# Softcapped attention with routed experts on one core: the score tile split into four one-bank tiles for the tail, and TensorE's share of the softmax sums cut to two head groups

## The chip, the cores and the metric

The kernel runs on one core of a Trainium2 chip. The metric is device time in microseconds, the median of several executions. The profile is of one further execution, taken by the hardware profiler.

## The reference, cut to what matters

Eight batches, twelve heads, 448 positions, head width 64. The attention output of a batch is a matrix of 448 rows and 768 columns. The router takes the 128 rows with the highest score, sends them through a two-layer network (768 to 1024 to 768), and adds the gated result to those rows.

```
scores = cap * tanh((q @ k.T) / sqrt(64) / cap)            # cap = 30
attn   = exp(scores - max); attn = attn / (sum(attn) + 1e-9)
x[b]   = attn @ v                                          # heads side by side: 448 x 768
s      = x[b] @ w_gate
top    = the 128 rows of largest s
out[b] = x[b];  out[b, top] += sigmoid(s[top]) * (relu(x[b, top] @ w1) @ w2)
```

With a cap of 30 the exponential needs no maximum taken off (the kernel tests the cap at run time and takes its fast branch); the sums are divided out at the end.

## The kernel before, in words

**Head groups and steps.** Four heads of one batch form a "double"; there are 24 doubles, three to a batch. A double has seven steps, each a block of 64 key positions for its four heads. Scores are kept transposed: key positions on the partitions, 448 queries along the row.

**The attention pipeline.** Two steps make a pair, 84 pairs in all. For a pair TensorE writes eight score matmuls (`scores_mm`, L372) into the tile `psS`, which is four PSUM banks in one tile; ScalarE takes tanh of all four banks in one instruction into a slot `p` (L842) and then the exponential in place (L850). There is one `psS`, so the scores of the next pair wait for the tanh of this one. Eight value matmuls a pair (`values_mm`, L381) accumulate into two banks, `psV`. The ring `p` has four slots.

**The sums.** The softmax sum over the key positions is taken in two ways (`sums_proc`). VectorE adds the steps of a double into a tile `e` (L400 the first addition, L410 the others), and TensorE sums `e` over the partitions with 16 small matmuls against a column of ones (L423). For some doubles the last two steps are left out of `e`, and TensorE sums them directly, 16 more matmuls of the same kind for each step. Before, that is done as long as the planner has no time yet for the last weight of `w2`.

**The rest of a double.** The sums are copied (`sm`), turned (L435) and inverted (`rec`, L443, L446); the value banks are copied to `xT` (L390), turned on TensorE (L469, banks `psT` and `psH`), scaled into `xn` by VectorE (L483), stored, and multiplied with the gate weights (L508). After three doubles of a batch the routing runs: totals (L530, L532), a turn (L542), a comparison of all rows with all (L557, L562), a one-hot matrix (L592), a picking matmul (L601), and an indirect DMA from GpSimd that gathers the rows (L625).

**The experts.** The gathered rows are turned (L641) and split into a high and a low part (L390, L653). The first layer is two groups of 18 matmuls (L698), the second two groups of 24 (L735), a VectorE instruction combines (L751), and an indirect DMA scatters (L777). The weights are split into high and low parts by VectorE as well (L325, L328), 14 pieces, in the first quarter of the run.

**What sets the order.** The program is written out beforehand by a planner inside the kernel (`Sim`, `Front`): every piece of work is a task with an engine, a planned duration and dependencies, and the planner emits instructions in the order in which its clocks reach them. Each engine then runs its list in that order; semaphores are set by the framework, per tile. `Front.policy` fills TensorE's time between attention steps with expert work and with the turns of finished doubles, at a rate that leaves a reserve for the time after attention. When the last value step is planned, `finish_attention` hands the banks of `psV` and the four banks of `psS` to the ring of free banks, so that the remaining expert work (the tail) has eight banks instead of two.

Of the kernel before, what the change touches and what calls it, by code (L numbers as in the profile page):

```python
# [8 lines left out]
F32 = mybir.dt.float32  # L9
# [7 lines left out]
P = 128  # L17
# [195 lines left out]
def allocate(tc, K):  # L213
    cp = K.const

    def t(name, shape, dt=F32):
        return cp.tile(shape, dt, name=name)

    S, CP, NCH = K.S, K.CP, K.NCH
    K.cap = t("capc", [P, 1])  # L220
    K.ident = t("ident", [P, P])
    K.fast = t("fast", [1, 1], I32)
    K.sq = t("sq", [1, 1])
    K.sc = t("sc", [P, 1])
    K.wts = {}
    for nm, n, m in (("w1", K.ND, K.F), ("w2", K.NF, K.DM)):
        for part in "hl":
            K.wts[nm + part] = t(nm + part, [P, n, m], F32R)
    K.wg = t("wg", [CP, K.DM])
    K.iota = t("iota", [CP, P])  # L230
    K.ids = t("ids", [CP, NCH])
    K.vals = [t(f"vals{i}", [CP, 4, NCH], F32R) for i in range(2)]
    K.before = t("before", [CP, S], BF16)
    K.ones = t("ones", [P, 63])
    K.part = [t(f"part{i}", [CP, K.NG, NCH]) for i in range(2)]
    K.jk, K.jt = t("jk", [CP, S], BF16), t("jt", [CP, S], BF16)
    K.work = K.stack.enter_context(tc.tile_pool(name="work", bufs=1))

    def ring(name, n, shape, dt=F32):
        return Ring([t(f"{name}{i}", shape, dt) for i in range(n)])  # L240

    K.q = ring("q", 3, [P, 2, S])
    K.k = ring("k", 3, [P, 2, S])
    K.v = ring("v", 2, [P, K.NS, 2, HD])
    K.p = ring("p", 4, [P, 2, 2, S])
    K.e = ring("e", 2, [P, 2, S])
    K.xT = ring("xT", 6, [P, S])
    K.sm = ring("sm", 2, [P, CP])
    K.xn = ring("xn", 2, [CP, NCH, 4 * K.D])
    K.rec = ring("rec", 2, [CP, NCH, 4])  # L250
    K.row = ring("row", 1, [CP, S])
    K.sel = ring("sel", 1, [CP, NCH, P], F32R)
    K.score = ring("score", 2, [CP, NCH])
    K.rk = ring("rk", 2, [CP, 3, NCH])
    K.xe = ring("xe", 2, [P, K.DM])
    K.idx = ring("idx", 3, [P, 1], I32)
    K.gt = ring("gt", 3, [P, 1])
    K.xs = Ring([(t("xh", [P, K.ND, P], F32R), t("xl", [P, K.ND, P], F32R))])
    K.hs = Ring([t("hs", [P, 1024])], free=False)
    K.hp = Ring([None], free=False)  # L260
    K.stages = [Ring([o]) for o in (K.hs.slots[0].obj, "mh", "ml")]

    def bank(tag, shape):
        pool = K.stack.enter_context(tc.tile_pool(name="ps" + tag, bufs=1, space=PSUM))
        return pool.tile(shape, F32, tag=tag, name="ps" + tag)

    K.S4 = bank("S", [P, 4, 512])
    K.acc = [Ring([bank(f"V{i}", [P, 512])]) for i in range(2)]
    K.banks = Ring([bank(c, [P, 512]) for c in "TH"])


def load_flag(tc, K, cap):
# [122 lines left out]
def sums_proc(tc, K, D):  # L395

    nc = tc.nc
    sim = K.sim
    yield [D.exp[0], D.exp[1]]
    e = yield Task("DVE", 1004, lambda t: nc.vector.tensor_tensor(  # L400
        t.slots[0].obj, D.P[0], D.P[1], op=ALU.add), deps=D.exp[:2], take=[K.e], refs=[1],
        reads=[D.pslot[0], D.pslot[1]], prio=1.5, kind="add")
    slot = e.slots[0]
    direct = []
    for s in range(2, K.NS):
        yield [D.exp[s]]
        if K.weights["w2"].t is None and s >= K.NS - 2:
            direct.append(s)
            continue
        e = yield Task("DVE", 1004, lambda t, s=s: nc.vector.tensor_tensor(  # L410
            slot.obj, slot.obj, D.P[s], op=ALU.add), deps=[e, D.exp[s]], reads=[D.pslot[s]],
            prio=1.5, kind="add")
    rec = K.recs[D.d]

    def sums(t):
        ps = t.slots[0].obj
        parts = [slot.obj] + [D.P[s] for s in direct]
        todo = [(part, n) for part in parts for n in range(K.NCH)]
        for i, (part, n) in enumerate(todo):
            for r in range(2):  # L420
                for j in range(2):
                    at = 32 * (2 * r + j)
                    nc.tensor.matmul(ps[at:at + 32, :K.CP], lhsT=K.ones[HALF[r], 31 - n:63 - n],  # L423
                                     rhs=part[HALF[r], j, n * K.CP:(n + 1) * K.CP],
                                     start=(i == 0), stop=(i == len(todo) - 1))

    s = yield Task("PE", 770 + 748 * len(direct), sums, deps=[e] + [D.exp[s] for s in direct],
                   take=[K.banks, K.sm], refs=[1, 1], shape=COLSUM,
                   reads=[slot] + [D.pslot[s] for s in direct], prio=(0, D.d), kind="sums")
    bank, sm = s.slots  # L430
    c = yield copy_task(tc, K.CP, lambda t: sm.obj, lambda t: bank.obj[:, :K.CP], deps=[s],
                        reads=[bank], prio=2, kind="smcopy")

    def turn(t):
        nc.tensor.transpose(t.slots[0].obj[:K.CP, :P], sm.obj, K.ident)  # L435

    t = yield Task("PE", 120, turn, deps=[c], take=[K.banks, K.rec], refs=[1, 2], reads=[sm],
                   prio=(0, D.d), kind="turnsums")
    tb, rec.slot = t.slots

    def scale(t):
        r = rec.slot.obj
        nc.vector.tensor_scalar(  # L443
            r, tb.obj[:K.CP, :P].rearrange("p (i r) -> p r i", i=4)[:, :K.NCH, :],
            1.0 + EPS, None, op0=ALU.mult)
        nc.vector.reciprocal(r, r)  # L446

    r = yield Task("DVE", 370, scale, deps=[t], reads=[tb], prio=1, kind="rec")
    rec.t = r.t
# [340 lines left out]
class Front:  # L790
# [216 lines left out]
    def finish_attention(self):  # L1007
        K = self.K
        self.over = True
        K.tail = True  # L1010
        for r in K.acc:
            for s in r.slots:
                s.ring = K.banks
                if s in r.free:
                    K.banks.free.append(s)
            r.free = []
        for i in range(4):
            s = Slot(K.banks, K.S4[:, i, :])
            s.t = self.S_free or self.sim.clock["ACT"]
            K.banks.free.append(s)  # L1020

# [24 lines left out]
def fast_path(tc, K, first, w1, w2):  # L1046
    nc = tc.nc
    sim = K.sim = FrontSim()
    plan(tc, K, K.B * K.NG)
    K.wprio = 1.5  # L1050
    Ds = [first] + [Double(K, d) for d in range(1, K.B * K.NG)]
    for nm in "qkv":
        Ds[1].load(tc, K, sim, nm)
    wg = sim.add(Task("SP", 700, lambda t: nc.sync.dma_start(
        K.wg, K.w_gate.partition_broadcast(K.CP)), lag=2000, prio=2, kind="wg"))
    K.wg_in = wg
    for D in Ds[2:]:
        for nm in "qkv":
            D.load(tc, K, sim, nm)
    load_consts(tc, K)  # L1060
    sim.spawn(weights_proc(tc, K, w1, w2))
    for D in Ds:
        sim.spawn(sums_proc(tc, K, D))
        sim.spawn(output_proc(tc, K, D))
    K.front = Front(tc, K, Ds)
    sim.policy = K.front.policy
    sim.run()


def first_loads(tc, K, D):  # L1070
# [56 lines left out]

def general_path(tc, K, w1, w2):
    nc = tc.nc
    rings = [K.q, K.k, K.v, K.p, K.e, K.xT, K.sm, K.xn, K.rec, K.row, K.sel, K.score, K.rk, K.xe,  # L1130
             K.idx, K.gt, K.xs, K.banks] + K.acc + K.stages
    for r in rings:
# [25 lines left out]
    for d in range(K.B * K.NG):  # L1158
        D = Double(K, d)
        for nm, src, ring in (("q", K.qd, K.q), ("k", K.kd, K.k), ("v", K.vd, K.v)):  # L1160
            ev = Event(0)
            ev.slots = [ring.slots[d % 2]]
            setattr(D, nm, ev)
            nc.sync.dma_start(D.at(nm), src[d])
        for s in range(K.NS):
            D.P[s] = K.p.slots[s // 2].obj[:, s % 2]
        D.accs = {i: K.acc[i].slots[0] for i in range(2)}
        for h in range(2):
            general_pair(tc, K, D, h)
        for s in range(K.NS):  # L1170
            values_mm(tc, K, D, s)
        now = max(sim.clock.values())
        for i in range(2):
            s = K.xT.next()
            K.xT.free.remove(s)
            s.refs = 1
            nc.vector.tensor_copy(s.obj, D.accs[i].obj[:, :K.S])
            D.x[i].slot, D.x[i].t = s, now
        r = K.rec.next()
        K.rec.free.remove(r)  # L1180
        r.refs = 2
        nc.vector.memset(r.obj, 1.0)
        K.recs[d].slot, K.recs[d].t = r, now
        sim.spawn(output_proc(tc, K, D))
        sim.wake()
        sim.run()


@with_exitstack
# [70 lines left out]
```

## Time and profile before

| | us |
|---|---|
| median of 3 runs | 516.25 (514.73 to 518.7) |
| the profiled execution | 514.5 |
| its span, first to last instruction | 512.8 |
| last value matmuls of attention start, tail begins | 441.8, 443.5 |
| last matmul of all ends | 505.8 |

The profile is read engine by engine: PE is TensorE's matmuls, PEld its weight loads, DVE VectorE, ACT ScalarE, POOL GpSimd, SP the queue of the plain DMAs. An fp32 matmul leaves two records, so eight score matmuls stand as x16. Ends of matmuls are modelled, so that "busy" PE may be waiting; what paces a stretch is better seen in when the next tanh starts.

### The profile page before, as it was taken

Reading aid. Unit: us, or ns where it says so; the run is one execution under the profiler, and the core shown is the slowest. Engines: PE = TensorE matmul, PEld = TensorE weight load, DVE = VectorE, ACT = ScalarE, POOL = GpSimd, SP = SyncE. Lnnn points to the kernel's source line nnn. Section 1 sums busy time; section 2 is a strip of 40 time slices with the busy share of each in tenths; the row PEclk is TensorE's granted clock in tenths of the full one; section 3 lists DMA queues with packets and bytes.
Section 4 is the critical chain, followed back from the end, with each engine's and each line's share of the span. In section 5 each row is a group of like instructions: output and inputs, shape, how many; then the busy total and the mean of one; then the engine's idle time right before and its main releaser. Section 6 shows DMA issues by size and latency. Waiting matters only on the chain.

```text
span 512.8 us, 11499 instructions
## 1 busy us (share of the span) xinstructions
PE 492.5 (96%) x4982; PEld 286.3 (56%) x4982; DVE 350.7 (68%) x826; ACT 320.6 (63%) x224; POOL 22.6 (4%) x26
## 2 busy tenths in 40 slices
PE   7999999999999999999999999999999999889984
PEld 4434545555454564555656465567455665578873
DVE  2496889879955687765667774797486957777320
ACT  5988979878768757588746968545776655102000
POOL 1000000100000000100100000001000100000100
PEclk9999999999999999999999999999999999999999
DMA  7865646354323342432423343324230202031100
GB/s 246 298 202 171 208 134 209 103 176 144 108 71 106 109 140 73 122 114 84 139 73 109 109 128 115 109 73 136 89 126 17 88 14 91 21 100 52 31 33 35
DMA packets 25674, 57.79 MB, mean 113 GB/s; under 512 B 2208, under 2 KB 13728, under 8 KB 25616
## 3 DMA queue, kind: packets, MB, share of 16 engines
q1 hardware_dynamic: 24336, 50.68, 31.1%
q0 software_dynamic: 1280, 6.29, 3.7%
q8 instruction: 41, 0.67, 0.6%
q14 instruction: 17, 0.14, 0.1%
HBM read 42.81 MB, written 14.16 MB: 111 GB/s over the span
## 4 chain that ended last, share of the span: by engine, by line
PE 88%; issue 4%; ACT 3%; DVE 2%; DMA 1%; SPq 0%; POOL 0%; POOLq 0%; ACTq 0%; DVEq 0%
PE psS L372 25%; PE psV L381 25%; PE psT L735 6%; PE psH L698 6%; PE psT L698 5%; PE psT L423 4%; PE psS L735 3%; PE psH L423 3%; PE psH L735 2%; ACT p L842 2%; PE psT L469 2%; PE psH L469 2%; PE psH L641 1%; PE psV L698 1%; PE psT L641 1%
## 5 line engine op out<-in xcount | busy, mean ns | idle before, releaser
L842 ACT ACTIVATE p<-psS,sc 128x1792 f32<-128x1792 f32 x84 | 147.7, 1758 | 88.4 <-PE psS L372 87.6
L850 ACT ACTIVATE p<-p,capc 128x1792 f32<-128x1792 f32 x84 | 150.7, 1795 | 2.2
L410 DVE TENSOR_TENSOR e<-e,p 128x896 f32<-128x896 f32 x106 | 115.0, 1085 | 52.9 <-ACT p L850 52.2
L372 PE MATMUL psS<-q,k 64*64 64x448 f32 x1344 | 143.3, 541 | 3.7 <-ACT p L842 3.3
L381 PE MATMUL psV<-p,v 64*64 64x448 f32 x1344 | 141.5, 541 | 0.4
L372 PEld LDWEIGHTS psS<-q,k 64*64 64x64 f32 x1344 | 49.4, 133 | 76.2 <-issue 51.0
L381 PEld LDWEIGHTS psV<-p,v 64*64 64x64 f32 x1344 | 48.2, 133 | 70.3 <-issue 64.6
L390 DVE COPY xT<-psV 128x448 f32<-128x448 f32 x38 | 22.7, 621 | 28.6 <-PE psV L381 27.3
L508 DVE CUSTOM_DVE_ANT_0 jk<-xn,wg 112x256 bf16<-112x256 f32 x96 | 40.2, 419 | 1.8
L625 POOL DMA_INDIRECT xe<-out,idx x8 | 12.1, 1518 | 325.6 <-DVE gt L611 325.6
L557 DVE TENSOR_SCALAR_CACHE_REDUCE jk<-row,score 112x448 bf16<-112x448 f32 x32 | 21.6, 674 | 0.4 <-ACT row L390 0.3
L400 DVE TENSOR_TENSOR e<-p 128x896 f32<-128x896 f32 x12 | 13.1, 1088 | 8.9 <-ACT p L850 6.9
L483 DVE TENSOR_TENSOR xn<-psT,rec 112x512 f32<-112x512 f32 x22 | 15.1, 686 | 1.5 <-PE psT L469 1.4
L562 DVE SCALAR_TENSOR_TENSOR jt<-row,score,before 112x112 bf16<-112x112 f32 (+3 forms) x32 | 15.8, 495 | 0.0
L483 DVE TENSOR_TENSOR xn<-psH,rec 112x512 f32<-112x512 f32 x21 | 14.4, 686 | 2.0 <-PE psH L469 1.8
L400 DVE TENSOR_TENSOR e<-p,p 128x896 f32<-128x896 f32 x12 | 13.0, 1082 | 3.7 <-ACT p L850 3.3
L777 POOL DMA_INDIRECT out<-xe,idx x8 | 8.5, 1059 | 155.5 <-DVE xe L751 147.4
L735 PE MATMUL psT<-w2h,hh 128*128 128x384 f32 x56 | 15.1, 367 | 0.0
L469 PE MATMUL psT<-ident,xT 128*112 128x128 f32 x88 | 13.7, 278 | 0.1
L735 PE MATMUL psT<-w2h,hl 128*128 128x384 f32 x56 | 13.7, 349 | 0.0
L735 PE MATMUL psS<-w2h,hh 128*128 128x384 f32 x40 | 10.3, 360 | 3.4 <-DVE hl L653 1.6
L423 PEld LDWEIGHTS psT<-e,ones 64*32 64x32 f32 x416 | 9.5, 106 | 7.2 <-issue 4.5
(180 smaller groups left out, 570.2 us busy)
## 6 DMA issues: line engine op xcount, KB each, us to landing
v<-in_v SPq DMA_DIRECT2D x24, 448.0 KB, 3.3
out<-xn SPq DMA_DIRECT2D x24, 448.0 KB, 3.6
q<-in_q SPq DMA_DIRECT2D x23, 448.0 KB, 3.5
k<-in_k SPq DMA_DIRECT2D x23, 448.0 KB, 4.8
stage<-in_moe_w SPq DMA_DIRECT2D x4, 512.0 KB, 8.1
stage<-in_moe_w SPq DMA_DIRECT2D x5, 384.0 KB, 3.4
hs<-in_moe_w SPq DMA_DIRECT2D x3, 384.0 KB, 3.0
hs<-in_moe_w SPq DMA_DIRECT2D x2, 512.0 KB, 7.3
```

The lines of the kernel that those rows point to most:

```text
L372: tc.nc.tensor.matmul(K.S4[HALF[r], 2 * i + j, :K.S], lhsT=k[HALF[j], r, s * HD:(s + 1) * HD], rhs=q[HALF[j], r, :], start=True, stop=True)
L381: tc.nc.tensor.matmul(D.accs[r].obj[HALF[j], :K.S], lhsT=v[HALF[r], s, j, :], rhs=p[HALF[r], j, :], start=(s == 0), stop=(s == K.NS - 1))
L400: e = yield Task("DVE", 1004, lambda t: nc.vector.tensor_tensor(t.slots[0].obj, D.P[0], D.P[1], op=ALU.add), deps=D.exp[:2], take=[K.e], r ...
L410: e = yield Task("DVE", 1004, lambda t, s=s: nc.vector.tensor_tensor(slot.obj, slot.obj, D.P[s], op=ALU.add), deps=[e, D.exp[s]], reads=[D ...
L423: nc.tensor.matmul(ps[at:at + 32, :K.CP], lhsT=K.ones[HALF[r], 31 - n:63 - n], rhs=part[HALF[r], j, n * K.CP:(n + 1) * K.CP], start=(i == ...
L469: nc.tensor.transpose(t.slots[0].obj[:CP, n * P:(n + 1) * P], x.slot.obj[:, n * CP:(n + 1) * CP], K.ident)
L483: nc.vector.tensor_tensor(xn.slot.obj[:, :, pair * P:(pair + 1) * P].rearrange("p c (h d) -> p c h d", d=K.D), bank.obj[:CP].rearrange("p ...
L508: nc.vector.tensor_tensor_reduce(out=K.jk[:, :W], in0=slot.obj[:, c, :], in1=K.wg[:, D.grp * W:(D.grp + 1) * W], scale=1.0, scalar=0.0, op ...
L698: nc.tensor.matmul(ph[:M], lhsT=(xh, xl)[part][:, i, :M], rhs=K.wts[r][:, i, fs], start=(n == 0), stop=(n == len(ops) - 1))
L735: nc.tensor.matmul(bank[0].obj[:M, :HH], lhsT=hp[0].obj[part][:, i, :M], rhs=K.wts[r][:, i, ds_], start=(start and n == 0), stop=(stop and ...
L842: nc.scalar.activation(slot.obj, K.S4.rearrange("p (i j) s -> p i j s", j=2) [:, :, :, :K.S], AF.Tanh, scale=K.sc)
L850: nc.scalar.activation(slot.obj, slot.obj, AF.Exp, scale=K.cap)
```

## The change

Two things are changed. The tile of the scores is no longer opened once for the whole kernel: it has a pool of its own, which is closed when attention ends; four tiles of one bank each, `psA` to `psD`, are opened in its place and given to the ring of banks. And a double's last two steps are summed directly on TensorE in doubles 0 and 1 only; in the order before, that was so in doubles 0 to 6. Lines after the new functions move down by 11 in the changed kernel.

```
-    def bank(tag, shape): ...
-    K.S4 = bank("S", [P, 4, 512])
+def open_scores(tc, K):
+    K.score_stack = ExitStack()
+    K.S4 = bank(tc, K.score_stack, "S", [P, 4, 512])
+
+def split_scores(tc, K):
+    K.score_stack.close()
+    K.score_stack = ExitStack()
+    return [bank(tc, K.score_stack, c, [P, 512]) for c in "ABCD"]
...
-        if K.weights["w2"].t is None and s >= K.NS - 2:
+        if D.d < 2 and s >= K.NS - 2:
             direct.append(s)
             continue
...
-        for i in range(4):
-            s = Slot(K.banks, K.S4[:, i, :])
+        for b in split_scores(self.tc, K):
+            s = Slot(K.banks, b)
```

Since the planner writes the program from these rules, its order moves from the third double on. On TensorE, around the sums of double 2 (`e_93`; `p_90`, `p_91` are the slots with its last two steps), before:

```order
L372 MATMUL psS<-q_81,k_84 64x448 x8
L381 MATMUL psV_131<-p_91,v_87 64x448 x2
L381 MATMUL psV_135<-p_91,v_87 64x448 x2
L423 MATMUL psT<-e_93,ones 32x112 x16
L423 MATMUL psT<-p_90,ones 32x112 x16
L423 MATMUL psT<-p_91,ones 32x112 x16
L372 MATMUL psS<-q_81,k_84 64x448 x8
L469 MATMUL psH<-ident,xT_97 112x128 x4
```

and now:

```order
L383 MATMUL psS<-q_81,k_84 64x448 x8
L392 MATMUL psV_127<-p_91,v_87 64x448 x2
L392 MATMUL psV_131<-p_91,v_87 64x448 x2
L480 MATMUL psT<-ident,xT_97 112x128 x4
L480 MATMUL psH<-ident,xT_98 112x128 x4
L383 MATMUL psS<-q_81,k_84 64x448 x8
L434 MATMUL psT<-e_93,ones 32x112 x16
L383 MATMUL psS<-q_81,k_84 64x448 x8
```

The 32 matmuls that read `p_90` and `p_91` are gone, and the 16 on `e_93` stand one pair of steps later.

On VectorE at the same double, from its fifth step on, before:

```order
L410 TENSOR_TENSOR e_93<-e_93,p_90 128x896
L443 TENSOR_SCALAR rec_106<-psH 112x16
L446 RECIPROCAL rec_106<-rec_106 112x16
L325 CAST w1h<-stage 128x1024
L328 TENSOR_TENSOR w1l<-stage,w1h 128x1024
L390 COPY xT_99<-psV_131 128x448
L325 CAST w1h<-stage 128x1024
L390 COPY sm_101<-psT 128x112
L328 TENSOR_TENSOR w1l<-stage,w1h 128x1024
L400 TENSOR_TENSOR e_94<-p_91,p_92 128x896
```

and now:

```order
L421 TENSOR_TENSOR e_93<-e_93,p_90 128x896
L454 TENSOR_SCALAR rec_106<-psH 112x16
L457 RECIPROCAL rec_106<-rec_106 112x16
L421 TENSOR_TENSOR e_93<-e_93,p_90 128x896
L336 CAST w1h<-stage 128x1024
L421 TENSOR_TENSOR e_93<-e_93,p_91 128x896
L401 COPY xT_99<-psV_127 128x448
L401 COPY xT_100<-psV_131 128x448
L494 TENSOR_TENSOR xn_104<-psT,rec_106 112x4x128
L494 TENSOR_TENSOR xn_104<-psH,rec_106 112x4x128
L339 TENSOR_TENSOR w1l<-stage,w1h 128x1024
```

Two more additions stand before the next weight piece, and the low part of that piece comes five rows later.

On TensorE in the tail, with the waits, around the turns of the last double (`xT_99`, `xT_100`), before:

```order
L469 MATMUL psS<-ident,xT_99 112x128 x4
L469 MATMUL psS<-ident,xT_100 112x128 x4
L735 MATMUL psS<-w2h,hl 128x384 [waits DVE_49]
L735 MATMUL psS<-w2h,hl 128x384
L735 MATMUL psS<-w2h,hh 128x384 x2
L735 MATMUL psS<-w2h,hh 128x384 [waits DVE_49]
```

and now:

```order
L480 MATMUL psV_131<-ident,xT_99 112x128 [waits DVE_49]
L480 MATMUL psV_131<-ident,xT_99 112x128 x3
L480 MATMUL psB<-ident,xT_100 112x128 [waits DVE_49]
L480 MATMUL psB<-ident,xT_100 112x128 x3
L746 MATMUL psA<-w2h,hl 128x384 x2
L746 MATMUL psA<-w2h,hh 128x384 x4
L746 MATMUL psA<-w2l,hh 128x384 x4
```

The second-layer matmuls, which had waits on VectorE in the middle of their group, have none here; the waits stand at the turns, which open a bank.

## Rows read from the trace of the kernel before

**Rows 1.** The page: busy time of the engines (share of the span, instructions), and the engines' shares of the chain that ended last.

```profile
PE 492.5 (96%) x4982; PEld 286.3 (56%) x4982; DVE 350.7 (68%) x826; ACT 320.6 (63%) x224; POOL 22.6 (4%) x26
...
PE 88%; issue 4%; ACT 3%; DVE 2%; DMA 1%; SPq 0%; POOL 0%; POOLq 0%; ACTq 0%; DVEq 0%
```

**Rows 2.** ScalarE's instructions in order of time, the tanh of seven pairs: start, duration, what it is, and in brackets the idle time before it and what ended it. Pairs are counted from 0; these are pairs 1, 2, 11, 14, 15, 33 and 83.

```profile
11.05 1.76 ACT L842 ACTIVATE p<-psS,sc 128x1792 f32<-128x1792 f32 x1
...
14.66 1.76 ACT L842 ACTIVATE p<-psS,sc 128x1792 f32<-128x1792 f32 x1
...
50.76 1.76 ACT L842 ACTIVATE p<-psS,sc 128x1792 f32<-128x1792 f32 x1 [0.64 <-PE psS L372]
...
62.98 1.76 ACT L842 ACTIVATE p<-psS,sc 128x1792 f32<-128x1792 f32 x1 [0.18 <-PE psS L372]
...
69.18 1.76 ACT L842 ACTIVATE p<-psS,sc 128x1792 f32<-128x1792 f32 x1 [2.62 <-PE psS L372]
...
151.19 1.76 ACT L842 ACTIVATE p<-psS,sc 128x1792 f32<-128x1792 f32 x1 [3.71 <-PE psS L372]
...
431.50 1.76 ACT L842 ACTIVATE p<-psS,sc 128x1792 f32<-128x1792 f32 x1 [1.12 <-PE psS L372]
```

**Rows 3.** The chain of waits in order of time, pieces on TensorE: start, duration, tile and line, number of records.

```profile
61.38 1.50 PE psS L372 x16
...
63.14 2.43 PE psT L423 x96
65.57 0.58 PE psH L469 x4
...
69.06 2.25 PE psV L381 x24
...
225.70 1.05 PE psT L735 x6
...
265.41 1.40 PE psT L698 x6
```

**Rows 4.** Busy time of the engines in stretches (length, then PE, PEld, DVE, ACT, POOL, each with its instructions, granted clock of TensorE, share and rate of the DMA engines): pairs 11 to 32, pairs 33 to 82, the tail, VectorE's stretch from the first addition of double 1 to that of double 9, and a stretch of 25 us in it.

```profile
50.76:151.19 100.43, 99.08 (x1315) 51.36 (x1311) 84.49 (x201) 80.07 (x53) 3.52 (x2) 1.00 0.46 147
151.19:431.50 280.31, 279.76 (x2674) 158.81 (x2670) 197.26 (x444) 189.62 (x132) 12.01 (x9) 1.00 0.31 98
443.49:505.84 62.35, 54.98 (x314) 47.58 (x314) 30.27 (x102) 5.64 (x12) 4.10 (x4) 0.97 0.16 49
26.76:148.02 121.26, 119.90 (x1598) 60.37 (x1591) 101.88 (x231) 101.36 (x65) 3.43 (x2) 1.00 0.49 158
...
50.00:75.00 25.00, 24.11 (x386) 12.71 (x382) 19.53 (x45) 20.24 (x14) 0.00 (x0) 1.00 0.53 166
```

**Rows 5.** The same view for VectorE alone, from the first addition of double 4 to that of double 5 (length, busy time, granted clock, DMA).

```profile
67.39:84.63 17.24, 16.35 (x41) 1.00 0.54 169
```

**Rows 6.** Groups of instructions by line, VectorE: number, then busy time, mean ns of one, idle time before it and its releaser.

```profile
L410 DVE TENSOR_TENSOR e<-e,p 128x896 f32<-128x896 f32 x106 | 115.0, 1085 | 52.9 <-ACT p L850 52.2
...
L508 DVE CUSTOM_DVE_ANT_0 jk<-xn,wg 112x256 bf16<-112x256 f32 x96 | 40.2, 419 | 1.8
...
L557 DVE TENSOR_SCALAR_CACHE_REDUCE jk<-row,score 112x448 bf16<-112x448 f32 x32 | 21.6, 674 | 0.4 <-ACT row L390 0.3
...
L562 DVE SCALAR_TENSOR_TENSOR jt<-row,score,before 112x112 bf16<-112x112 f32 (+3 forms) x32 | 15.8, 495 | 0.0
```

**Rows 7.** Who waited for whom in the tail (443.4 to 506 us), TensorE's weight loads: total us, times, longest.

```profile
PEld psS L735 <- DVE xn L483: 2.3, 3, 1.1
PEld psS L735 <- DVE hl L653: 2.1, 2, 1.1
PEld psS L735 <- DVE hh L390: 1.7, 2, 1.2
PEld psS L735 <- DVE xe L751: 1.5, 2, 1.0
PEld psS L735 <- DVE gt L619: 1.1, 1, 1.1
PEld psS L435 <- ACT hh L390: 0.9, 1, 0.9
PEld psS L735 <- DVE rec L443: 0.5, 1, 0.5
```

**Rows 8.** All engines in order of time, four rows of the tail: two weight loads with the idle time before them, and the last two instructions.

```profile
457.70 0.30 PEld L735 LDWEIGHTS psS<-w2h,hl 128*128 128x128 f32 x2 [1.03 <-DVE xn L483]
...
503.81 0.30 PEld L735 LDWEIGHTS psS<-w2h,hh 128*128 128x128 f32 x2 [1.03 <-DVE xe L751]
...
505.88 0.62 DVE L751 SCALAR_TENSOR_TENSOR xe<-psS,gt,xe 128x384 f32<-128x384 f32 x1 [2.12 <-PE psS L735]
506.78 0.98 POOL L777 DMA_INDIRECT out<-xe,idx  x1 [19.75 <-DVE xe L751]
```

**Rows 9.** TensorE in stretches of 2 us of the tail: length, busy time, granted clock, DMA.

```profile
458.00:460.00 2.00, 1.22 (x6) 0.94 0.00 0
460.00:462.00 2.00, 2.00 (x8) 0.50 0.63 175
462.00:464.00 2.00, 1.76 (x10) 0.71 0.17 58
```

**Rows 10.** The gathers of expert rows (L625), all eight: from issue to landing.

```profile
DMA to landing us min/median/max: 3.8/4.7/6.4
```

More of the change, by code (lines that the diff above doesn't have):

```diff
@@ L261, in allocate, with bank @@
     K.stages = [Ring([o]) for o in (K.hs.slots[0].obj, "mh", "ml")]
-    def bank(tag, shape):
-        pool = K.stack.enter_context(tc.tile_pool(name="ps" + tag, bufs=1, space=PSUM))
-        return pool.tile(shape, F32, tag=tag, name="ps" + tag)
-    K.S4 = bank("S", [P, 4, 512])
-    K.acc = [Ring([bank(f"V{i}", [P, 512])]) for i in range(2)]
-    K.banks = Ring([bank(c, [P, 512]) for c in "TH"])
+    K.acc = [Ring([bank(tc, K.stack, f"V{i}", [P, 512])]) for i in range(2)]
+    K.banks = Ring([bank(tc, K.stack, c, [P, 512]) for c in "TH"])
+def bank(tc, stack, tag, shape):
+    pool = stack.enter_context(tc.tile_pool(name="ps" + tag, bufs=1, space=PSUM))
+    return pool.tile(shape, F32, tag=tag, name="ps" + tag)
+def open_scores(tc, K):
[5 more added lines that the diff above has]
+    return [bank(tc, K.score_stack, c, [P, 512]) for c in "ABCD"]
 def load_flag(tc, K, cap):
@@ L1066, in fast_path @@
     sim.policy = K.front.policy
+    open_scores(tc, K)
     sim.run()
+    K.score_stack.close()
 def first_loads(tc, K, D):
@@ L1129, in general_path @@
     nc = tc.nc
+    open_scores(tc, K)
     rings = [K.q, K.k, K.v, K.p, K.e, K.xT, K.sm, K.xn, K.rec, K.row, K.sel, K.score, K.rk, K.xe,
@@ L1186, in general_path @@
         sim.run()
+    K.score_stack.close()
 @with_exitstack
```

## The prediction

> **What bounds the kernel now.** I read the page first: TensorE is busy 96% of the span and holds 88% of the chain, the next engine is VectorE with 68% [rows 1]. Busy matmuls may be waiting, so the second view is the start of each tanh, 84 of them. Where nothing is in the way, one pair follows the last after 3.61 us (14.66 less 11.05), which is ScalarE's own work, tanh and exponential; with something in the way the gap grows, and its bracket names the score matmuls (62.98 to 69.18 is 6.20 us, 2.62 of it idle) [rows 2].
>
> The third view is the chain on TensorE, which gives prices: eight score matmuls 1.50 us, twelve value matmuls 2.25 (eight 1.50), 48 summing matmuls 2.43 or 0.81 for 16, four turns 0.5, six matmuls of the first expert layer 1.40 or 0.234 each, six of the second 1.05 or 0.175 each [rows 3]. With these prices I added up, from the order, what TensorE does between one pair's scores and the next. For pairs 11 to 32 that is 94.7 us, and there are 32 changes between attention and other work; the stretch took 100.4 [rows 4], so a change costs some 0.18 us and ScalarE sets almost nothing there. For pairs 33 to 82 it is 266.8 plus 72 changes, 279.8, against 280.3 measured [rows 4]. So from pair 11 to the end of attention the kernel is paced by TensorE's work, and a gap is the larger of 3.61 us and that work.
>
> The last view is the tail. By the same prices it has 50.3 us of TensorE work, and it lasts 62.35 [rows 4]. The waits account for the rest: twelve weight loads into psS wait, 10.1 us together [rows 7], and the granted clock falls to 0.50 (1.2 GHz) after a stretch in which TensorE worked 1.22 of 2 us; over six microseconds that loses 0.06 x 2 + 0.50 x 2 + 0.29 x 2 = 1.7 us [rows 9]. 50.3 + 10.1 + 1.7 is 62.1.
>
> **The change part by part.** *The sums.* Five doubles (2 to 6) lose two direct steps each: 160 matmuls, ten times 0.81 is 8.1 us of TensorE's work. VectorE gains ten additions of 1085 ns, 10.9 us [rows 6].
>
> *What moves with them.* The planner finishes the weights a good double later, and the expert work starts at pair 32 or 33 where it started at pair 28. So three stretches have to be counted apart.
>
> Pairs 0 to 10 are the same in both orders. In pairs 11 to 32 the work falls from 94.7 to 75.8 us: 8.1 for the sums, 8.2 for 35 first-layer matmuls, 2.6 for some turns, all but the sums put off. With 35 changes at 0.18 that is 82.1. But now ten of the 22 pairs have less work than the 3.61 us of ScalarE, and the shortfall adds up to 3.4: 85.5 instead of 100.4, so -14.9 us. The bounds of that shortfall: nothing, if the order lets pairs run into each other, and the 19.5 us of the first rival below, if VectorE falls behind; I take 3.4, from the row nearest to it, the 3.61 us pair.
>
> In pairs 33 to 82 the work rises by 17.2 us (53 more first-layer matmuls are 12.4, one more sum 0.8, turns and picks 4.0), all of it in a stretch that TensorE paces: +17.2. From the last scores to the last values the work is 0.9 less. The tail has 24 second-layer matmuls fewer (4.2) and four each of three kinds of turns and picks (1.4): 44.7 instead of 50.3, -5.6. Together the work part is -14.9 + 17.2 - 0.9 - 5.6 = -4.2 us, which is the 8.1 saved less the new idle time.
>
> *The split tile.* In [rows 8] a second-layer matmul waits 1.03 us for VectorE's scaling of xn, whose result it doesn't read, and another 1.03 for the combination of the other half. What they share is the tile: the framework sets its semaphores per tile, and psS is four banks in one. In the new order these matmuls write psA or psB, and the waits in the middle of their groups are gone. What is late next are two gathers: the last one has 26 second-layer matmuls and four turns to hide behind, 5.0 us, against 0.5 for the index and 3.8 to 6.4 from issue to landing [rows 10], so 0 to 1.9 of wait, and the first one about as much. The true chain of the last expert (turn, two VectorE passes of 0.69) has 18 matmuls, 3.2 us, before its reader and stays hidden. The waits that remain are therefore between 0 and 10.1; I take 2.0, nearer to the row of the gathers: -8.1 us.
>
> The Trainium skill (PSUM — Partial Sum Buffer, section "PSUM bank collisions raise a hardware error") asks for a semaphore between two engines per bank and quadrant, and calls different banks clean. By that rule the chip needs none of the waits on another bank, and the sum would be up to 10.1; it leaves those between users of one bank. The rows agree in that the named readers and the waiting matmul use different banks; no run so far shows the four banks as tiles of their own.
>
> *The clock.* The fall stands right behind three of those waits, TensorE idle for 0.78 of 2 us [rows 9]; with them gone I count its 1.7 us back, at worst it stays. The Trainium skill (TensorE: Matmul & The Clock Gate, section "What's actually happening") has the half clock as the idle state that activity lifts; by it the 1.7 go with the idle time, which is what I take from the rows.
>
> *The pool.* Closing and opening it is no instruction; the new tiles wait for the last tanh. The first matmul into psA stands behind the value matmuls of that same pair, which need its exponential, so that is free; without that cover it costs one tanh, 1.76 us [rows 2]. The loads on SP's queue keep their number; a weight piece that waits for VectorE holds up the q, k and v behind it, which come three doubles ahead of use.
>
> **The sum.** -4.2 - 8.1 - 1.7 = -14.0. The profiled execution took 514.5 us (span 512.8, and the 7 us behind the last matmul stay: the combination at 505.88, the scatter at 506.78 [rows 8]), so 500.5. The median of the runs shown is 1.75 above that execution: 502 us.
>
> **The rivals.** *VectorE sets the early pace.* From the first addition of double 1 to that of double 9 it was busy 101.9 of 121.3 us, 84% [rows 4]. By the new order it has 10.9 more and 12.2 less there (four score reductions, four comparisons of each kind and others go later [rows 6]), so 100.6, and by the count above the stretch shrinks to 109.5: 92%. It was at 95% in one double before [rows 5], so it can be packed so; but over 50 to 75 us it was at 78% [rows 4], waiting for others. If it gets no better than 78%, the stretch takes 129.0, 19.5 more than counted, tanh waits for slots of p that the additions still hold, and the time is 521.5, slower than before. From 81% downwards the change loses. Against it: by the same prices each of these doubles' sums stands in the new order 7 us or more behind the moment at which VectorE, without a pause, would be through with its work up to them. Chance 0.07.
>
> *The tail's waits stay or come back elsewhere.* If the four tiles take over the waits (one bank reused soon, the gathers late), 8.1 and 1.7 are not won: 512. For it: the tail's work is a chain of small steps on three engines; against it: the readers named in [rows 7] are mostly others than the matmul needs. Chance 0.09.
>
> *The saving in the early stretch all turns into waiting for ScalarE.* It also takes copies (sm, xT, 0.25 to 0.5 each), so that a pair may need 3.9 instead of 3.61; ten short pairs and a few more would lose 6 us: 508. Chance 0.09.
>
> **How the numbers follow.** My forecast, 502, has 0.75. Its own range is 497 (no shortfall, no wait left: 3.4 + 2.0 less) to 508. The range of 8 in 10 reaches up to the tail rival, 512, and down to 495, where the median lies as low as the profiled execution did. A difference of 1% is 5.2 us, about what a measurement of this kernel can tell from none: faster by that means below 511.1, which holds for the forecast and the ScalarE rival, 0.84; the tail rival at 512 is within 1%, 0.09; VectorE's is slower, 0.07.
>
> **What would show it.** In the new profile: tanh starts some 15 us earlier at pair 33 (about 136), most of it gone by pair 83 (431 to 434); sums with p as input in four groups of 16 only; a tail of 46 to 48 us with no wait on psA to psD in the middle of a second-layer group, and a clock of 1.00 in it. VectorE over 90% busy from 27 to 136 us. I am wrong in the first part if tanh waits for VectorE between pairs 11 and 33, and in the second if the tail takes 55 us or more.

## The result, and the profile after

The changed kernel takes 496.98 us (median of 4 runs, 496.68 to 497.49), the kernel before 515.49 beside it (514.32 to 518.7): ratio 0.9632, 95% interval 0.9586 to 0.9678, faster by 3.2 to 4.1%. The profiled execution took 496.79 us, with a span of 495.0. Of all executions below one, of the second run without direct sums, took 1685.66 us and is in no ratio.

The page, as in [rows 1], busy time and the chain that ended last:

```profile
PE 481.2 (97%) x4662; PEld 276.4 (56%) x4662; DVE 361.3 (73%) x836; ACT 320.3 (65%) x224; POOL 22.4 (5%) x26
...
PE 85%; DVE 6%; ACT 4%; issue 4%; DMA 1%; POOL 0%; POOLq 0%; DVEq 0%; ACTq 0%
```

TensorE has 320 records less, the 160 matmuls of the sums, and 11.3 us less busy time. VectorE has ten instructions and 10.6 us more, and its share of the chain rose from 2% to 6%: it now stands closer to the path. The same tanh as in [rows 2], pairs 11, 33 and 83, in ScalarE's order of time:

```profile
50.64 1.75 ACT L853 ACTIVATE p<-psS,sc 128x1792 f32<-128x1792 f32 x1 [0.62 <-PE psS L383]
...
135.56 1.75 ACT L853 ACTIVATE p<-psS,sc 128x1792 f32<-128x1792 f32 x1 [0.53 <-PE psS L383]
...
432.60 1.75 ACT L853 ACTIVATE p<-psS,sc 128x1792 f32<-128x1792 f32 x1 [1.15 <-PE psS L383]
```

Pair 33 comes 15.6 us earlier than before and pair 83 comes 1.1 later. So the whole early gain is paid back by the expert work that was put off, and what the kernel keeps lies behind attention. The stretches in the order of [rows 4] (VectorE's stretch from the first addition of double 1, pairs 11 to 32, pairs 33 to 82, the tail; columns as there):

```profile
26.76:136.00 109.24, 105.89 (x1251) 45.75 (x1247) 102.37 (x202) 100.33 (x63) 1.11 (x1) 1.00 0.54 170
50.64:135.56 84.92, 81.57 (x937) 34.93 (x933) 81.40 (x168) 78.62 (x51) 1.11 (x1) 1.00 0.52 163
135.56:432.60 297.04, 296.79 (x2795) 172.49 (x2791) 216.39 (x513) 191.98 (x136) 14.40 (x10) 1.00 0.30 96
444.14:488.90 44.76, 44.74 (x278) 40.47 (x277) 23.88 (x73) 4.92 (x10) 2.92 (x3) 1.00 0.17 55
```

In the tail TensorE is busy 44.74 of 44.76 us at a granted clock of 1.00: nothing is left there but work, as far as modelled ends can tell. The waits of its weight loads in the tail, the answer to [rows 7]:

```profile
PEld psA L746 <- PE psV L392: 0.7, 1, 0.7
PEld psH L434 <- issue: 0.2, 1, 0.2
PEld psA L746 <- issue: 0.2, 1, 0.2
```

No wait on VectorE or ScalarE is left of twelve. The two gathers, in all engines' order of time, each with the first weight load that reads it, and the last two instructions of the kernel:

```profile
440.15 0.97 POOL L636 DMA_INDIRECT xe<-out,idx  x1 [29.93 <-DVE gt L622]
...
444.69 0.14 PEld L652 LDWEIGHTS psC<-ident,xe 128*128 128x128 f32 x1
...
462.88 0.97 POOL L636 DMA_INDIRECT xe<-out,idx  x1 [8.82 <-DVE gt L622]
...
467.12 0.14 PEld L652 LDWEIGHTS psC<-ident,xe 128*128 128x128 f32 x1
...
488.92 0.62 DVE L762 SCALAR_TENSOR_TENSOR xe<-psV,gt,xe 128x384 f32<-128x384 f32 x1 [1.47 <-PE psV L746]
489.82 0.97 POOL L788 DMA_INDIRECT out<-xe,idx  x1 [16.65 <-DVE xe L762]
```

The readers come 4.5 and 4.2 us behind the gathers, which took 3.8 and 3.9 us to land, and have no bracket: they waited for nothing.

### The profile page after: what moved, and what is told of

It reads as the page before. It is cut to its first block, busy times and chain, and to the rows that moved or that the text cites. A ratio compares the mean times of both kernels' runs of the same rounds, so it can differ in the third digit from the quotient of the medians.

```text
span 495.0 us, 10878 instructions
## 1 busy us (share of the span) xinstructions
PE 481.2 (97%) x4662; PEld 276.4 (56%) x4662; DVE 361.3 (73%) x836; ACT 320.3 (65%) x224; POOL 22.4 (5%) x26
## 4 chain that ended last, share of the span: by engine, by line
PE 85%; DVE 6%; ACT 4%; issue 4%; DMA 1%; POOL 0%; POOLq 0%; DVEq 0%; ACTq 0%
PE psS L383 24%; PE psV L392 23%; PE psH L709 6%; PE psT L709 5%; PE psH L746 5%; PE psT L746 5%; ACT p L853 3%; PE psT L434 3%; DVE e L421 2%; PE psH L480 2%; PE psA L746 2%; PE psT L480 2%; PE psT L652 2%; PE psH L434 1%; PE psD L709 1%
## 5 line engine op out<-in xcount | busy, mean ns | idle before, releaser
L421 DVE TENSOR_TENSOR e<-e,p 128x896 f32<-128x896 f32 x116 | 125.6, 1083 | 44.4 <-ACT p L861 43.8
L519 DVE CUSTOM_DVE_ANT_0 jk<-xn,wg 112x256 bf16<-112x256 f32 x96 | 40.3, 420 | 1.9
L636 POOL DMA_INDIRECT xe<-out,idx x8 | 11.3, 1416 | 285.6 <-DVE gt L622 285.6
L411 DVE TENSOR_TENSOR e<-p,p 128x896 f32<-128x896 f32 x12 | 13.1, 1088 | 9.5 <-PE psT L434 6.7
L494 DVE TENSOR_TENSOR xn<-psH,rec 112x512 f32<-112x512 f32 x24 | 16.5, 687 | 4.2 <-PE psH L480 3.8
L722 ACT ACTIVATE hs<-psT 128x512 f32<-128x512 f32 x7 | 4.1, 591 | 23.2 <-PE psT L709 23.2
L434 PEld LDWEIGHTS psT<-e,ones 64*32 64x32 f32 x512 | 11.7, 106 | 10.8 <-DVE xT L401 4.2
L434 PE MATMUL psT<-e,ones 64*32 64x112 f32 x512 | 15.5, 259 | 0.0
L480 PE MATMUL psH<-ident,xT 128*112 128x128 f32 x96 | 14.8, 276 | 0.5 <-DVE sm L401 0.5
L722 ACT ACTIVATE hs<-psH 128x512 f32<-128x512 f32 x8 | 4.8, 595 | 16.0 <-PE psH L709 16.0
L709 PE MATMUL psH<-w1h,xh 128*128 128x512 f32 x48 | 14.9, 419 | 0.0
```

What stands on the lines that cost most here:

```text
L480: nc.tensor.transpose(t.slots[0].obj[:CP, n * P:(n + 1) * P], x.slot.obj[:, n * CP:(n + 1) * CP], K.ident)
L519: nc.vector.tensor_tensor_reduce(out=K.jk[:, :W], in0=slot.obj[:, c, :], in1=K.wg[:, D.grp * W:(D.grp + 1) * W], scale=1.0, scalar=0.0, op ...
L709: nc.tensor.matmul(ph[:M], lhsT=(xh, xl)[part][:, i, :M], rhs=K.wts[r][:, i, fs], start=(n == 0), stop=(n == len(ops) - 1))
```

## The experiments

The runs stand on three chips. The kernel before ran beside them: 514.63 us with the four runs from the split alone to the weights split twice, 514.52 with the second run of the changed kernel, the second without direct sums and the two with casts on GpSimd, 515.93 with the others. Ratios are to these; a difference in us from the changed kernel's 496.98 crosses chips, between which the kernel before differs by up to 1.4 us.

**The tile.** Each edit alone, and a split half as fine.

Split only: the changed kernel with the old rule of the sums.

```
-        if D.d < 2 and s >= K.NS - 2:
+        if K.weights["w2"].t is None and s >= K.NS - 2:
```

> The split tile alone; the sums stay as before (doubles 0 to 6 summed directly in their last two steps), and so does the order up to the end of attention. By my theory (the semaphores of the one tile made ten microseconds of waits in the tail, and the half clock stands behind them): tanh of pair 33 at 151 us and of pair 83 at 431.5 us as before, tail 50 to 52 us instead of 62.4, no wait of psA to psD in the middle of a second-layer group, clock 1.00 in the tail. Time 514.5 - 10.1 - 1.7 = 502.7, between 501 and 505. Rival, that the tail's waits are true ones and that the shorter tail came from the new order: 512 to 515, with the waits on other tiles.

Measured: 502.21 us (501.92 to 506.5, 5 runs), ratio 0.9768 (0.9732 to 0.9804). Its tail, from the end of the last value matmuls to the last matmul of all, and its weight loads that wait there:

```profile
447.69:498.56 50.87, 50.63 (x314) 46.04 (x314) 29.91 (x102) 5.62 (x12) 4.10 (x4) 1.00 0.19 60
```

```profile
PEld psA L746 <- issue: 0.9, 2, 0.7
PEld psV L709 <- ACT xh L401: 0.5, 1, 0.5
PEld psT L434 <- issue: 0.2, 1, 0.2
```

The same 314 records that took 62.35 us in [rows 4] take 50.87, with a clock of 1.00. The order of work is the old one, so the waits and the half clock belonged to the tile; the rival, true waits, is out. The one wait on another engine that is left, 0.5 us for `xh`, is a true one: the first layer reads `xh`. Also gone are the waits whose releaser wrote `hh` or `hl`, 3.8 of the 10.1 us of [rows 7], though a second-layer matmul reads tiles of these names. The profiled execution, 506.5 us, began late by some 3.6 us (last section): its pairs 33 and 83 stand at 155.40 and 435.70, with the 280.3 us between them as before.

Sums only: the kernel before with the new rule.

```
-        if K.weights["w2"].t is None and s >= K.NS - 2:
+        if D.d < 2 and s >= K.NS - 2:
```

> The change of the sums alone (direct in doubles 0 and 1); the scores' tile stays one tile of four banks to the end. By my theory the stretches up to the end of attention are those of the changed kernel: tanh of pair 33 at 135 to 137 us, of pair 83 at 432 to 434. The tail has 44.7 us of TensorE work and the waits of the one tile, some eight to ten of 1 us in the middle of groups, and may have the half clock for 1 to 2 us: 54 to 57 us. Time 505 to 509. Rival, that the waits came from the old order of the tail and not from the tile: 496 to 498. A third view, that the two edits overlap and this one alone already brings all: also 497.

Measured: 506.01 us (505.81 to 507.97, 4 runs), ratio 0.9855 (0.9814 to 0.9896). Tanh of pair 33 and of pair 83 stand 0.15 us from the changed kernel's. The tail, and the weight loads that wait in it:

```profile
444.30:497.89 53.59, 47.26 (x277) 40.16 (x277) 24.12 (x73) 4.83 (x10) 2.93 (x3) 1.00 0.14 46
```

```profile
PEld psS L735 <- DVE xn L483: 2.5, 2, 1.4
PEld psS L735 <- DVE xl L653: 1.5, 2, 1.0
PEld psS L698 <- DVE xe L751: 1.1, 1, 1.1
PEld psS L735 <- DVE hh L390: 1.1, 1, 1.1
PEld psS L698 <- DVE row L390: 1.0, 1, 1.0
PEld psS L735 <- DVE xh L390: 1.0, 1, 1.0
...
PEld psS L641 <- DVE xl L653: 0.7, 1, 0.7
PEld psS L735 <- DVE hl L653: 0.5, 1, 0.5
```

In the new order too the one tile makes waits: these rows add up to 9.4 us, and the tail is 8.8 longer than with four tiles. Most of these matmuls do not read what VectorE made there (the second layer reads neither xn nor xl nor xh, the first neither xe nor row); they only share the tile. The clock stayed at 1.00 through these ten waits of 0.5 to 1.4 us, also where TensorE worked 1.22 of 2 us as it did in [rows 9] before the fall:

```profile
452.00:454.00 2.00, 1.22 (x8) 0.90 (x7) 1.36 (x4) 0.00 (x0) 0.00 (x0) 1.00 0.00 0
```

So the 1.7 us of clock before belonged to one spot of the old order and not to the tile as such.

Two tiles of two banks in place of four of one:

```
-    return [bank(tc, K.score_stack, c, [P, 512]) for c in "ABCD"]
+    two = [bank(tc, K.score_stack, c, [P, 2, 512]) for c in "AB"]
+    return [t[:, i, :] for t in two for i in range(2)]
```

> The changed kernel, but with two tiles of two banks each instead of four tiles of one bank. By my theory (a wait for each pair of users that share a tile, whatever bank they use) some of the waits come back: the order has about as many waits of second-layer matmuls in the middle of a group as with one tile, seven or eight, but their releasers then share only one other bank, so I expect half the time, 3 to 7 us of waits in the tail: 500 to 504. Rival, that it is only the one tile that also holds the scores: no waits, 497.

Measured: 501.74 us (501.23 to 503.42, 4 runs), ratio 0.9766 (0.9726 to 0.9807). Its tail and its waits (its lines stand one further down):

```profile
445.92:493.79 47.87, 45.78 (x277) 40.32 (x277) 23.94 (x73) 4.93 (x10) 2.93 (x3) 1.00 0.16 51
```

```profile
PEld psA L747 <- DVE xn L495: 1.1, 1, 1.1
PEld psB L710 <- DVE row L402: 1.0, 1, 1.0
PEld psA L747 <- PE psV L393: 0.7, 1, 0.7
...
PEld psB L653 <- DVE xl L665: 0.7, 1, 0.7
PEld psA L747 <- DVE hl L665: 0.5, 1, 0.5
```

The four waits on VectorE add up to 3.3 us, within the 3 to 7 that were expected, though there are four of them and not seven or eight. With the same work the tail is 44.8, 47.9 and 53.6 us for four, two and one tiles: the wait grows with the number of banks that share a tile, as the theory has it. Of the 5.1 us between the profiled spans, 500.1 and 495.0, 3.1 lie in the tail and 1.7 in the first pairs (last section); how the other executions began is not known.

**VectorE.** The rival with which the change would have lost. The order of TensorE is the same in these three.

Weights split twice (the calls alone, shortened; each stands in a task of the planner, whose planned durations stay):

```
-    nc.vector.tensor_copy(hi, st[:, :m])
+    [nc.vector.tensor_copy(hi, st[:, :m]) for _ in range(2)]
...
-    nc.vector.tensor_tensor(lo, st[:, :m], hi.bitcast(F32), op=ALU.subtract)
+    [nc.vector.tensor_tensor(lo, st[:, :m], hi.bitcast(F32), op=ALU.subtract) for _ in range(2)]
```

> The changed kernel with VectorE's split of the weights done twice (each cast and each subtraction issued two times, the second time with the same result); the order of every other instruction is the same. From 26.8 to 136 us VectorE gains 3 pieces of w1 at 1.9 us and 8 of w2 at 1.5, 17.7 us, and it was busy 102.4 of 109.2. If it has no room there but the 6.8 us, as its 98% between 80 and 110 us says, the pair 33 comes 11 to 14 us later, tanh waits for VectorE, and nothing of it is got back later: 508 to 512. That would say that the first rival of the prediction was missed by some six microseconds of VectorE's work. Rival, that its instructions have time to slide since the sums stand 7 us behind: 497 to 500.

Measured: 516.72 us (514.2 to 517.81, 10 runs), ratio 1.0037 (1.001 to 1.0064): all that the change had won is gone, and more than the 508 to 512 that was expected. The stretch up to pair 33, which comes at 153.25, then one sum on TensorE that waits for an addition, and TensorE in steps of 2 us around it:

```profile
26.80:153.25 126.45, 112.28 (x1247) 49.64 (x1243) 123.45 (x228) 100.10 (x63) 1.12 (x1) 0.95 0.45 147
```

```profile
121.19 1.16 PE L434 MATMUL psT<-e,ones 64*32 64x112 f32 x20 [4.20 <-DVE e L421]
```

```profile
117.00:119.00 2.00, 0.00 (x0) 0.00 (x0) 2.00 (x3) 0.75 (x2) 0.00 (x0) 1.00 0.07 27
119.00:121.00 2.00, 0.00 (x0) 0.00 (x0) 1.97 (x6) 0.00 (x0) 0.00 (x0) 0.85 0.00 0
121.00:123.00 2.00, 1.81 (x36) 1.48 (x40) 1.97 (x7) 0.00 (x0) 0.00 (x0) 0.50 0.91 234
...
127.00:129.00 2.00, 2.00 (x14) 0.78 (x17) 1.93 (x6) 0.97 (x1) 0.00 (x0) 0.50 0.89 323
129.00:131.00 2.00, 2.00 (x20) 0.72 (x16) 1.97 (x6) 1.88 (x2) 1.12 (x1) 0.59 0.48 155
```

VectorE is busy 97.6%, and the place of the wait is the sum of a double: TensorE takes its instructions in order, so the 16 matmuls that need `e` stop everything behind them; a tanh waits up to 6.5 us for its scores. 17.7 us of work made pair 33 17.7 later, where 11 to 14 was expected. TensorE did nothing from 117 to 121 us, and then ran at half its clock (1.2 GHz) to about 130, while VectorE worked on without a pause.

The casts alone twice, 6.5 us:

> As the kernel with the weights split twice, but only the casts are done twice (0.67 us for a piece of w1, 0.56 for one of w2): from 26.8 to 136 us VectorE gains 3 x 0.67 + 8 x 0.56 = 6.5 us, just less than the 6.8 it was idle there. With the weights split twice it stood at 123.45 of 126.45 us, 97.6% busy. If 97.6% is the limit, the stretch becomes (102.4 + 6.5) / 0.976 = 111.6 us instead of 109.2: 2.4 later, plus 1 to 2 if TensorE is put to its lower clock behind a wait: 499 to 501. Rival, that each added microsecond costs one, as the 17.7 added cost 17.7 to 20: 503. Third, that the first 6.8 are free: 497.

Measured: 500.85 us (499.96 to 503.1, 4 runs), ratio 0.9734 (0.9692 to 0.9776), 3.9 over the changed kernel. Up to its pair 33, at 138.79, and the sum that waits:

```profile
26.80:138.79 111.99, 106.14 (x1247) 45.76 (x1243) 108.83 (x215) 99.88 (x62) 1.12 (x1) 1.00 0.52 166
```

```profile
122.19 0.49 PE L434 MATMUL psH<-e,ones 64*32 64x112 f32 x12 [1.30 <-DVE e L421]
```

The first reading, a limit near 97.6%, holds: VectorE is at 97.2%, and of the 6.5 us about half is hidden and half, 3.2 us at pair 33, costs time.

The other way, VectorE relieved: the casts on GpSimd (the call alone, shortened).

```
-    nc.vector.tensor_copy(hi, st[:, :m])
+    nc.gpsimd.tensor_copy(hi, st[:, :m])
```

> The changed kernel with the 14 casts of the weights (0.56 to 0.67 us each on VectorE) issued on GpSimd, which is 5% busy; TensorE's order is the same. VectorE is relieved of 6.5 us between 26.8 and 136 us. If VectorE does not pace the changed kernel's early stretch (TensorE's work and ScalarE's 3.6 us a pair do, which gave 85.5 us for pairs 11 to 32 against 84.9 measured), pair 33 comes at 135 to 136 as before and the time is 497. If VectorE's 94% holds it up after all: pair 33 at 132 to 134, 494. If the two engines disturb each other, or the subtraction waits for a slow cast: 500 or more.

Measured: 497.25 us (495.24 to 497.45, 5 runs), ratio 0.9653 (0.9628 to 0.9677), against 497.1 for the changed kernel on the same chip: the same. Pair 33 comes at 135.28. So VectorE is just not what holds the changed kernel; from the run before, in which 3.3 of 6.5 us found room, it stands some 3 us from the edge.

**The sums.** Direct sums in other doubles, all with four tiles; the edit is the number in `D.d < 2`. All 24 doubles (`D.d < 24`):

> The changed kernel with direct sums in all 24 doubles: 44 more steps on TensorE, 44 x 0.81 = 35.7 us, and 44 additions less on VectorE, 47.7 us. By my theory (TensorE's work paces everything, 0.81 a step): 496.8 + 35.7 less some of the idle time in the early stretch (2 to 3) = 529 to 532. Rival, that VectorE holds up the kernel so that its relief counts: under 520.

Measured: 530.17 us (529.37 to 530.97, 2 runs), ratio 1.0288 (1.024 to 1.0337). 33.2 us more for 44 steps, 0.75 each, 2.5 less than the 35.7 counted. About 2 of that is early idle time: TensorE stood idle 1.3 us between pair 11 and pair 33, against 3.35 in the changed kernel. So a step summed on TensorE costs about its work, as expected.

Four doubles (`D.d < 4`):

> The changed kernel with direct sums in doubles 0 to 3 instead of 0 and 1: TensorE gains 64 matmuls, 3.25 us, VectorE loses four additions, 4.3 us. By TensorE's work: pair 33 at 139 us instead of 135.6, and the sum comes out 3 later, 499 to 500. Rival, that VectorE's 94% costs the changed kernel something that is won back here: 496 or less.

Measured: 504.45 us (503.23 to 505.41, 4 runs), ratio 0.9791 (0.9752 to 0.983). That is 7.5 over the changed kernel, where 3 was expected. Pair 33 came at 138.2, as expected, and pair 83 at 428.0, 4.6 before the changed kernel's; but from there to the end of the span the kernel takes 74.2 us, against 62.4 in the changed one, since more work is left for the tail: 7.2 more in all. TensorE from pair 50 to pair 83, first in the changed kernel and then here:

```profile
234.52:432.60 198.08, 197.84 (x1861) 115.95 (x1857) 141.51 (x338) 127.15 (x90) 9.16 (x7) 1.00 0.29 92
```

```profile
234.00:428.00 194.00, 191.51 (x1773) 113.82 (x1773) 136.14 (x311) 123.71 (x88) 8.95 (x7) 1.00 0.28 89
```

TensorE is idle for 2.5 us here against 0.24: the order has pairs with too little to fill them. That is a good half of the 4 us beyond the 3.25 counted. Over the whole run TensorE is idle 1.3 us more and busy 5.9 more, 487.1 against 481.2; why its busy time grew by 2.7 more than the sums is open.

No direct sums at all (`D.d < 0`); the same once more; and the changed kernel once more beside it:

> The changed kernel with no direct sums at all, also not in doubles 0 and 1: TensorE loses 64 more matmuls, 3.25 us, in pairs 5 to 11, and VectorE gains four additions, 4.3 us, between 20 and 44 us. By TensorE's work alone tanh of pair 11 comes at 48.7 us (before that 50.6), of pair 33 at 133 (135.6), of pair 83 at 424.6 (432.6, since 5 us of work go to the tail): 494. By VectorE (20.55 of 23.9 us busy between 26.7 and 50.6, and 95 to 98% from 50.6 to 110, so that what is pushed on has no room there) the 4.3 us more are not hidden: pair 33 at 136 to 139 and 497 to 500. After the run with the weights split twice I hold the second to be likelier.

> The kernel without any direct sums once more, to see whether its 495.57 us lies below the changed kernel on the same chip. If the 1.4 us are real: 495.3 to 496.2, with no overlap with the changed kernel's times. If they were chip to chip: within 0.5 us of it.

> The changed kernel once more, beside the kernel without direct sums on the same chip: 497.0, between 496.5 and 497.8.

Measured: 495.57 us the first time (495.56 to 495.96, 4 runs), ratio 0.962 (0.9587 to 0.9653); on the second chip 497.67 us (495.71 to 498.37 in four executions, and the one of 1685.66; without it the median is 497.36), ratio 0.967 (0.9645 to 0.9694), and the changed kernel beside it 497.1 us (496.84 to 498.69, 5 runs), ratio 0.9664 (0.964 to 0.9687). The profiled spans are 493.8 and 494.0 against 495.0 and 495.4, so a microsecond may be real, but the medians do not show it: no difference that these runs can tell. That VectorE would hold up the early stretch, which I had thought likelier, did not happen: pair 33 came at 133.2, where TensorE's work puts it, and waited for its score matmuls.

```profile
133.20 1.75 ACT L853 ACTIVATE p<-psS,sc 128x1792 f32<-128x1792 f32 x1 [0.48 <-PE psS L383]
```

Both, no direct sums and the casts on GpSimd:

> No direct sums, and the casts on GpSimd. Without direct sums tanh waited for TensorE 8.7 us between 20 and 160 us, and pair 33 came at 133.2, as TensorE's work alone gives (133); so VectorE's relief should bring nothing: 495.5, pair 33 at 132.5 to 133.5. If VectorE held it up: 493 to 494.

Measured: 497.93 us (495.46 to 498.56, 5 runs), ratio 0.9659 (0.9631 to 0.9686): nothing gained, and 2.4 over the 495.5 that was expected. Its profiled execution began late (pair 1 at 12.69, pair 33 at 136.44), but from pair 11 to pair 33 it took 84.7 us, against 84.4 with no direct sums alone. No version tried is clearly faster than the changed kernel.

## Why the prediction was right, and where a size was off

The prediction said 502 and the measurement says 496.98; direction and mechanism held, and the terms were these, from profile to profile (span 512.8 to 495.0, -17.8 where -14.0 was predicted):

| stretch | predicted | measured |
|---|---|---|
| pairs 11 to 32 | -14.9 | -15.5 |
| pairs 33 to 82 | +17.2 | +16.7 |
| last scores to last values | -0.9 | -0.45 |
| tail: work | -5.6 | -6.1 |
| tail: waits and clock | -8.1 - 1.7 | -11.5 |
| behind the last matmul | 0 | -0.9 |

The tail's two parts are told apart by the split alone: 62.35 to 50.87 us in the same order, then 44.76 in the new one. Pair 11 comes 0.1 us earlier, which is the rest.

**Pacing.** That TensorE's work, with the 3.61 us of ScalarE under it, paces attention was right to 0.6 us or better in each stretch. The order's rows priced by [rows 3] were enough for this change, but not for four direct doubles, where the same count missed 4 us. (Four turns are priced there at 0.5 us, where their row reads 0.58; that is 0.08 us for each four turns that moved.) Of the idle time that the new order was to have in pairs 11 to 32, 3.4 us, the larger part is there: TensorE's rose from 1.35 us (99.08 busy of 100.43) to 3.35 (81.57 of 84.92). The third rival, 6 us lost to ScalarE, did not come.

**The tile.** The mis-sized term is the remaining wait. The prediction left 2.0 us in the tail for the gathers, and measured are none: both readers come 4.2 us or more behind the gather and have no wait. So the tail took 44.8 us, less than the 46 to 48 foretold. That the count of the tail's work (44.7) is the tail (44.76) shows the rest of the term. By the split alone the tile is worth 12.4 us in the old order (514.63 to 502.21; 9.8 predicted), by the difference of sums only and the changed kernel 9.0 in the new one (506.01 to 496.98, on two chips). The rule of the Trainium skill that was weighed there (PSUM — Partial Sum Buffer, section "PSUM bank collisions raise a hardware error": different banks are clean) gave up to 10.1 for the waits alone. The runs agree with it: with tiles of one bank no wait on another engine was left in the changed kernel's tail, one of 0.5 us in that of the split alone, and the time of the waits went with them.

**The clock.** The 1.7 us came back, the tail's clock is 1.00. Right before the fall stood two waits, of 1.03 and 1.10 us (weight loads at 457.70 and 459.46); the next before them, of 0.46 us, ended at 454.19, so the three that the prediction put right before the fall are two. That the half clock comes with TensorE's idle time was shown once more with the weights split twice, 4 us of nothing and then 0.50, and ten waits of about 1 us with the sums alone did not bring it about. The Trainium skill (TensorE: Matmul & The Clock Gate, section "What's actually happening") calls the half clock the idle state; the first agrees, and the second says that not every pause leads there.

**The sums.** -4.2 us of work predicted for the rest; 5.2 measured between the split alone and the changed kernel (502.21 to 496.98, on two chips). Alone, with the one tile, they brought 8.6, so the two edits overlap: 12.4 + 8.6 is 21.0, and both together give 18.5. The one tile costs less in the new order, 9.4 us of waits and no clock against 10.1 and 1.7, so there is less for the split to save.

**The first rival.** It did not come, so its price, 521.5 us at a share of 78%, was not measured; its chance, 0.07, was low for how near it lay. VectorE's share came out at 94% in its stretch (102.4 of 109.2), where the prediction had 92%, and it can be packed to 97 or 98%. 6.5 us more of work there cost 3.2 at pair 33, and 17.7 cost the whole gain. That its sums stand 7 us behind fits: with 6.5 us added, one sum was late, by 1.3.

**The end.** The difference from median to profiled execution, 1.75 us added, did not carry over: the changed kernel's median is 0.2 above its profile. With the 3.8 us of the table it makes the miss of 5. The forecast's own range ended at 497, with no idle time in the early stretch and no wait left; that the measured 496.98 stands at that end is in part luck, since most of the idle time was there and the lower median took its place.

## What to carry to other kernels

When banks of PSUM change hands between users on different engines, give each its own tile: a wait whose releaser wrote something that the waiter doesn't read is the sign. The sum of such rows alone can be too low a price: here they made 6.3 of the 10.1 us, the others went with them, and with the clock the tail fell by 11.5. Work taken off the engine that paces a stretch is worth its time only if nothing later takes the place: here 15.5 us of early gain turned into 16.7 us of later work, and the net was read only by adding up the whole run. Before work is moved to a second engine, look at that engine's share in the stretch, not in the span: 73% in the page was 94% where it counted.

## What the runs showed that was not expected

The first pairs take a different time from one execution to the next: in the fourteen profiled executions the tanh of pair 1 starts at 10.9 to 11.3 us, but at 12.66 with two tiles of two banks, at 12.69 with no direct sums and casts on GpSimd, and at 14.55 with the split alone. That is probably part of the spread of the times. TensorE's first scores of the second pair, in the changed kernel and then in the profiled execution of the split alone:

```profile
9.11 1.74 PE L383 MATMUL psS<-q,k 64*64 64x448 f32 x16 [1.91 <-ACT p L853]
```

```profile
11.22 3.27 PE L383 MATMUL psS<-q,k 64*64 64x448 f32 x16 [1.91 <-ACT p L853]
```

The same eight matmuls took nearly twice as long, and the tanh of pair 1 came 3.6 us later (14.55 against 10.94); that execution took 506.5 us, its four others about 502. Its first eight score matmuls had begun 0.6 us later, behind a load of `q`, and took 3.79 us against 2.31. The granted clock reads 1.00 in both; the cause is open. So stretches of two executions are best compared by their lengths, not by their starts.

GpSimd's casts of the weights took 1.4 us for 128x768, where VectorE needs 0.56 (over both runs with such casts, group means from 0.83 to 1.54 us; spans on GpSimd are rough):

```profile
L336 POOL CAST w2h<-stage 128x768 fp32r<-128x768 f32 x5 | 7.1, 1411 | 39.9 <-DMA stage<-in_moe_w 39.9
```

VectorE's own work was slowed little, by the mean over the whole run: its additions took 1088 ns instead of 1083, its gate reductions (L519) 434 instead of 420.
